# PV of both heads of a pair in one PSUM bank: 64 output rows each, three products side by side, and x split straight from PSUM

## The chip, the cores and the metric

The kernel runs on one core of a Trainium2 chip. The metric is device time in microseconds (us) of one execution. The core's engines work side by side, each on its own queue in order: TensorE (PE, with its weight loads PEld), VectorE (DVE), ScalarE (ACT), GpSimd (POOL) and the queue that issues the DMAs (SP). Results of PE land in PSUM, in banks of 512 fp32 columns on 128 partitions.

## The reference

Attention with a forget gate over 8 batches, 8 heads, 576 positions and head width 64, then a two-layer network with g = h cos(h) on the joined heads:

```python
scores = scale * np.matmul(q, k.transpose(0, 1, 3, 2))
cum = np.cumsum(np.log(np.clip(f, 0.0001, 1.0)), axis=-1)
scores = np.where(causal, -1000000000.0, scores + cum[:, :, :, None] - cum[:, :, None, :])
attn = np.exp(scores - np.max(scores, axis=-1, keepdims=True))
attn = attn / (np.sum(attn, axis=-1, keepdims=True) + 1e-09)
x = np.matmul(attn, v)            # (8, 8, 576, 64) -> x: (4608, 512)
h = x @ w_in                      # w_in (512, 2048)
out = (h * np.cos(h)) @ w_out     # w_out (2048, 512)
```

To keep fp32 accuracy the kernel splits an fp32 number into two fp16 numbers, hi and lo, and adds up products of the parts.

## The kernel before, in words

**Units.** Two heads make a pair; four pairs (n = 4b to 4b+3) make batch b, and there are 32 pairs. For each head `attention(n)` computes scores for five row blocks of 128 positions on PE (lines 621 and 622, fp32 operands), adds the mask and takes the row minimum of the negated scores on DVE (632), takes exp and its sum on ACT (637), forms the reciprocal of the sum on POOL and DVE (642, 645) and splits the normalized P into fp16 hi (654, ACT) and lo (658, DVE) in the SBUF tiles PS3 (row blocks 3 and 4) and PS2 (0, 1, 2). A transposing DMA (663) brings them into `pt3` and `pt2` with the key position on partitions.

**PV.** V of a pair is split into hi and lo in the tile `vv` (584, 586). The 576 positions are cut into two halves of 320 and 256 columns (`UW`). For each head and each half, lines 671 to 689 multiply: the stationary operand is `vv[:, jb, hd]` as 128 columns, 64 of V hi and 64 of V lo, and the moving operand is P hi and then P lo of that head. So a bank receives P times V hi in rows 0 to 63 and P times V lo in rows 64 to 127: all four products of the parts. For a half of 320 a head takes 8 matmuls of 64, 256, 256 and 128 columns, two of each; for a half of 256 it takes 10, eight of 256 and two of 128.

**Behind PV.** ACT copies rows 64 to 127 into the tile `low` (694). For the first six pairs (`n < NX`) ACT also copies rows 0 to 63 into `x32` (698) and POOL adds `low` (700); from the seventh pair on DVE does scale and addition in one instruction that reads the bank (703). When both heads of a half are there, ACT casts `x32` to fp16 (713: xh) and POOL subtracts (715: xl).

**The network.** For each of 16 units u (a half of a batch) `gemm1` multiplies xh and xl with the split w_in (735), ACT brings h out of PSUM (740), DVE and ACT compute h cos(h) (749, 751, 753, 755) and split it (757 gh, 758 gl), and `gemm2` multiplies with the split w_out (775), whose result leaves through ACT (780) and a DMA. The weights come as 64-bit numbers; DVE puts fp32 words together from them at the start (428, 432, 436), ACT takes their sums (447), and after a maximum over partitions (`allmax`, 380 to 385) each block of 512 columns is split: hi on ACT (456), lo on DVE (463) or on POOL (460 and 461).

**What sets the order.** All operations are recorded with an engine, a cost and a priority. `Plan.order()` then runs a list scheduler over them 20 times, forward and backward in turn, and keeps the shortest plan; the program's order on each engine is that plan's. An operation with `alt` is put on DVE or on POOL by which would finish it earlier in the plan: lines 574 and 575 (`sub`), 463 against 460 and 461, and 758. Rings of buffers (`BUFS`) limit how far work runs ahead: `pa1` has three PSUM banks that scores and PV share, `hp` three banks for the network (and, in the first three pairs, for the second head), `x32` and `low` one buffer each.

The loop at the end of the kernel advances a pair's generator by pieces:

```python
        adv(n)
        if p == 2 and b + 1 < B:
            prep_vscale(b + 1, float(n))
        adv(n)
        adv(n + 1)
        adv(n)
```

Of the kernel before, what the change touches and what calls it, by code (L numbers as in the profile page):

```python
# [13 lines left out]
F32 = mybir.dt.float32  # L14
F32R = mybir.dt.float32r
F16 = mybir.dt.float16
BF16 = mybir.dt.bfloat16
I32 = mybir.dt.int32
AF = mybir.ActivationFunctionType
ALU = mybir.AluOpType  # L20
# [4 lines left out]
P = 128  # L25
B, H, S, D = 8, 8, 576, 64
# [4 lines left out]
U0, UW = (0, 320), (320, 256)  # L31
NU = len(UW)
UM = max(UW)
QP = 640
NSET = 3
OFF = {0: 0, 1: 128, 2: 384, 3: 0, 4: 512}
# [1 line left out]
VS0 = -3.0  # L38
RAWS = {1: ("h",), 2: ("gh", "gl")}
SLQ, SLW, SLG = 2.0, 2.0, 0.0  # L40
NX = 6
LEAD = 2.0
NHP = 3
ROUNDS = 20
SWITCH = 4.0
TWO_PI = 2.0 * np.pi
NEG = -8.0e9
BUFS = dict(stage=2, x32=1, v2=2, vv=2, pt3=2, pt2=2, low=1, xh0=6, xl0=6, xh1=7, xl1=7, h=3, r=1, gh=5, gl=5, ot=1,
            pa2=1, pa1=3, hp=3, dg=1)


# [62 lines left out]
class Plan:  # L114
# [14 lines left out]
    def op(self, eng, cost, fn, reads=(), writes=(), prio=0.0, size=0, table=None, alt=None):  # L129
        o = Op()  # L130
        o.eng, o.cost, o.size, o.table, o.fn, o.prio, o.alt, o.id = eng, cost, size, table, fn, prio, alt, len(self.ops)
        deps = {}
        for b in reads:
            if b.last is not None:
                deps[b.last.id] = b.last
        for b in writes:
            if b.last is not None:
                deps[b.last.id] = b.last
            for r in b.readers:
                deps[r.id] = r  # L140
        for b in (*reads, *writes):
            r = b.root()
            assert not r.closed, r.name
            if r.wait:
                r.wait.closed = True
                for w in r.wait.ops:
                    deps[w.id] = w
            if r.prev is not None and r.prev.ops:
                deps[r.prev.ops[0].id] = r.prev.ops[0]
            r.ops.append(o)  # L150
        for b in reads:
            b.readers.append(o)
        for b in writes:
            b.last, b.readers = o, []
        deps.pop(o.id, None)
        o.deps, o.succ, o.n, o.ready = list(deps.values()), [], len(deps), 0.0
        for d in o.deps:
            d.succ.append(o)
        self.ops.append(o)
        return o  # L160
# [121 lines left out]
def c_dve(n, fast=False, k=1):  # L282
    return k * 0.064 + n * (0.53e-3 if fast else 1.06e-3)


def c_act(n, psum=False, aps=0):
    return (0.052 if psum else 0.093) + n / 1200.0 + 0.093 * aps


def c_pool(n):  # L290
    return 0.06 + n * 2.6e-3


def c_mm(n):
    return max(0.028, n / 2400.0 + 0.0025)
# [7 lines left out]
def fox_moe_kernel(ctx: ExitStack, tc: tile.TileContext, qkT, vp, fT, w1, w2, out):  # L303
# [51 lines left out]
    def ring(name, shape, dt, space=pool, tag=None):  # L355
        tag = tag or name
        return pl_.ring(tag, lambda: space.tile(shape, dt, name=tag, bufs=BUFS[tag]))

# [13 lines left out]

    def allmax(src, n, reads, dst, writes, pr):

        dg = ring("dg", [P, n, P], BF16, tag="dg" if n == 1 else "x32")
        pm = ring("hp", [P, 512], F32, psum)

        def spread():
            for j in range(n):
                V.tensor_scalar(dg.get()[:, j], eye, src()[:, j:j + 1], None, op0=ALU.mult)  # L380

        op("DVE", 0.2 * n, spread, reads=reads, writes=[dg], prio=pr)
        op("PE", c_mm(n * P) + 0.1, lambda: T.matmul(pm.get()[:, 0:n * P], ones, dg.get().rearrange("p n c -> p (n c)"), start=True, stop=True),
           reads=[dg], writes=[pm], prio=pr)
        op("DVE", c_dve(n * P), lambda: V.tensor_reduce(dst(), pm.get()[:, 0:n * P].rearrange("p (n c) -> p n c", n=n), axis=AX.X, op=ALU.max),
           reads=[pm], writes=writes, prio=pr)
# [166 lines left out]
    def attention(n):  # L553
# [37 lines left out]
        for hd in range(2):  # L591
# [11 lines left out]
            for tag, blocks in GROUPS:  # L603
# [10 lines left out]
                def mm(blocks=blocks, big=big, view=view, hi=hi, co=co):  # L614
                    for ib, o, w in blocks:
                        isl = slice(ib * P, ib * P + P)
                        hf = S // 2
                        d_ = view(ib, o, w)
                        for c, d in ((d_[:, 0], slice(0, hf)), (d_[:, 1], slice(hf, S))) if big else ((d_, slice(0, w)),):
                            d = slice(64 + d.start, 64 + d.stop)  # L620
                            T.matmul(c, hi[:, 0, isl], hi[:, 1, d], start=True, stop=False)  # L621
                            T.matmul(c, co[0:68, 0, isl], co[0:68, 1, d], start=False, stop=True)  # L622
# [42 lines left out]
                       reads=[PB[ib, hl] for ib in ibs for hl in range(2)], writes=[t], prio=pr + 0.2, size=int(nblk * 0.112 * DMA_BW))  # L665
            yield

        x32 = ring("x32", [P, S], F32)
        for hd in range(2):
            hs = slice(64 * hd, 64 * hd + 64)  # L670
            for half in range(NU):
                b0, w = U0[half], UW[half]
                pv = ring("hp" if n < NHP and hd == 1 else "pa1", [P, 512], F32, psum)
                t = (T2, T3)[half][hd]
                if half == 0:
                    jobs = [(0, 0, 0, 1, 64), (0, 64, 1, 3, 0), (1, 64, 1, 3, 0), (2, 192, 2, 3, 0)]
                else:
                    jobs = [(0, 0, 0, 2, 0), (1, 0, 0, 2, 0), (2, 0, 0, 2, 0), (3, 0, 0, 2, 0), (4, 128, 1, 2, 0)]

                def mm(pv=pv, t=t, jobs=jobs, hd=hd, half=half, w=w):  # L680
                    for k, (jb, o, i0, i1, c0) in enumerate(jobs):
                        first = k == 0 or (half == 0 and k == 1)
                        for hl in range(2):
                            bl = [OFF[3 * half + i] // P + jb for i in range(i0, i1)]
                            m = t.get()[:, hl, bl[0]:bl[-1] + 1:bl[-1] - bl[0] or 1, c0:]
                            o1 = o + (i1 - i0) * (P - c0)
                            d = pv.get()[:, o:o1].rearrange("p (a c) -> p a c", a=i1 - i0)
                            T.matmul(d, vv.get()[:, jb, hd].rearrange("p h d -> p (h d)"), m,  # L688
                                     start=(first and hl == 0), stop=(hl == 1 and (k == len(jobs) - 1 or (half == 0 and k == 0))))

                rd_ = [t, vv.part(0), vv.part(1)]
                op("PE", sum(2 * (c_mm((i1 - i0) * (P - c0))) for _, _, i0, i1, c0 in jobs) + 0.02, mm, reads=rd_, writes=[pv], prio=pr + 0.6)
                low, ls = ring("low", [P, UM], F32), hs if n < NX else slice(0, 64)
                op("ACT", c_act(w, True), lambda pv=pv, low=low, w=w, ls=ls: A.activation(
                    low.get()[ls, 0:w], pv.get()[64:128, 0:w], AF.Copy, scale=float(2.0 ** -14)), reads=[pv], writes=[low], prio=pr + 0.6)
                xp = x32.part((half, hd))
                if n < NX:
                    op("ACT", c_act(w, True), lambda pv=pv, hs=hs, b0=b0, w=w: A.activation(
                        x32.get()[hs, b0:b0 + w], pv.get()[0:64, 0:w], AF.Copy, scale=float(2.0 ** -14)), reads=[pv], writes=[xp], prio=pr + 0.6)
                    op("POOL", c_pool(w) + 0.06, lambda low=low, hs=hs, b0=b0, w=w: G.tensor_tensor(  # L700
                        x32.get()[hs, b0:b0 + w], x32.get()[hs, b0:b0 + w], low.get()[hs, 0:w], op=ALU.add), reads=[low], writes=[xp], prio=pr + 0.6)
                else:
                    op("DVE", c_dve(w), lambda pv=pv, low=low, hs=hs, b0=b0, w=w: V.scalar_tensor_tensor(
                        x32.get()[hs, b0:b0 + w], pv.get()[0:64, 0:w], float(2.0 ** -14), low.get()[0:64, 0:w], op0=ALU.mult, op1=ALU.add),
                       reads=[pv, low], writes=[xp], prio=pr + 0.6)
            if hd == 0:
                yield
        X.setdefault(n, [])
        for half in range(NU):
            b0, w = U0[half], UW[half]  # L710
            xh, xl = ring(f"xh{half}", [P, w], F16), ring(f"xl{half}", [P, w], F16)
            x3 = [x32.part((half, hd)) for hd in range(2)]
            op("ACT", c_act(w), lambda xh=xh, b0=b0, w=w: A.copy(xh.get(), x32.get()[:, b0:b0 + w]), reads=x3, writes=[xh],  # L713
               prio=pr + 0.6)
            op("POOL", c_pool(w), lambda xh=xh, xl=xl, b0=b0, w=w: G.tensor_tensor(xl.get(), x32.get()[:, b0:b0 + w], xh.get(), op=ALU.subtract),  # L715
               reads=[*x3, xh], writes=[xl], prio=pr + 0.6)
            X[n].append((xh, xl))

    GT = {}

# [142 lines left out]
```

## Time and profile before

| | |
|---|---|
| time, median of 3 runs | 1196.62 us (1196.18 to 1203.8) |
| profiled execution, its own time | 1195.68 us |
| its span, first to last instruction | 1194.0 us |
| PE busy | 1020.9 us, 86% |
| ACT busy | 936.1 us, 78% |
| DVE busy | 881.4 us, 74% |
| POOL busy | 400.5 us, 34% |
| mean granted TensorE clock | 0.947 |

The span and the profiled execution's own time differ by 1.7 us, so what is read from the span holds for the time. A matmul's duration in the profile is its latency; matmuls overlap, and their rate is read from a stretch of many of them. Rows of the groups give busy us and mean ns of one instruction, then the idle time just before it and what ended that. A row of the stretches gives the time from and to, its length, busy us with the number of instructions for PE, PEld, DVE, ACT and POOL, the granted clock, the DMA share and GB/s. A row of the waits gives who waited for whom, us in total, how often, and the longest.

### The profile page before, as it was taken

The numbers are of one execution on the slowest core, as the hardware profiler recorded it, in microseconds if no ns is written. First come the engines' busy times: TensorE is split into PE (matmuls) and PEld (weight loads), VectorE is DVE, ScalarE is ACT, GpSimd is POOL, SyncE is SP. The second block draws the span as 40 slices with busy tenths as digits, with TensorE's granted clock in tenths as the row PEclk, the third lists the DMA queues.
The fourth block names the chain that finished last, engine by engine and source line by source line (L and its number), as shares of the span: only waits on it lengthen the run. The fifth ranks groups of instructions, "written<-read, shape, count | busy, mean of one in ns | idle before, by whom it ended". The sixth has DMA issues, their size and how long they took to land. (4 is left out here: it accounts for less than half of the span.)

```text
span 1194.0 us, 22292 instructions
## 1 busy us (share of the span) xinstructions
PE 1020.9 (86%) x8077; PEld 826.3 (69%) x8077; DVE 881.4 (74%) x1879; ACT 936.1 (78%) x1922; POOL 400.5 (34%) x460
## 2 busy tenths in 40 slices
PE   1354348898999799989999899989989899999998
PEld 1243236677877687778877687777777777788777
DVE  4999997978578775878587866869497877863613
ACT  2688668999789887999699977989699888973523
POOL 3436667742422411253125221441135222200000
PEclk9975569999999999999999899999999999999999
DMA  9999834584637843696449544784459564440000
GB/s 256 276 281 274 219 89 82 134 200 99 152 77 192 191 85 70 156 197 141 104 97 232 122 100 81 169 209 102 88 134 205 111 152 103 84 78 15 6 23 19
DMA packets 291070, 161.25 MB, mean 135 GB/s; under 512 B 255056, under 2 KB 263248, under 8 KB 290960
## 3 DMA queue, kind: packets, MB, share of 16 engines
q1 hardware_dynamic: 290960, 159.83, 57.5%
q8 instruction: 63, 1.03, 0.4%
q14 instruction: 47, 0.39, 0.1%
HBM read 76.82 MB, written 10.62 MB: 73 GB/s over the span
## 5 line engine op out<-in xcount | busy, mean ns | idle before, releaser
L735 PE MATMUL hp<-xh,W1s 128*128 128x256 f16 (+1 forms) x2048 | 390.9, 290 | 16.6 <-ACT h L740 11.5
L775 PE MATMUL hp<-gh,W2s 128*128 128x256 f16 (+1 forms) x2048 | 381.9, 287 | 3.9 <-ACT h L740 3.3
L735 PEld LDWEIGHTS <-W1s 128*128 128x128 f16 x3072 | 298.3, 99 | 109.0 <-issue 30.5
L775 PEld LDWEIGHTS <-W2s 128*128 128x128 f16 x3072 | 296.4, 98 | 79.2 <-issue 5.3
L735 PE MATMUL hp<-xl,W1s 128*128 128x256 f16 (+1 forms) x1024 | 296.5, 290 | 2.2 <-POOL xl L715 2.2
L775 PE MATMUL hp<-gl,W2s 128*128 128x256 f16 (+1 forms) x1024 | 293.3, 286 | 0.3 <-DVE gl L758 0.2
L642 POOL TENSOR_SCALAR ri<-L 128x2 f32<-128x2 f32 (+1 forms) x192 | 67.7, 353 | 361.9 <-ACT pa L637 350.0
L658 DVE SCALAR_TENSOR_TENSOR PS<-pa,ri,PS 128x64 f16<-128x64 f32 (+4 forms) x308 | 154.6, 545 | 36.0 <-ACT PS L654 35.0
L637 ACT ACTIVATE pa<-pa,nb 128x64 f32<-128x64 f32 (+4 forms) x308 | 155.6, 505 | 26.9 <-DVE nb L632 24.9
L688 PEld LDWEIGHTS <-vv 128*128 128x128 f16 x1152 | 107.0, 103 | 85.7 <-issue 53.2
L632 DVE CUSTOM_DVE_ANT_0 pa<-pa,mask 128x64 f32<-128x64 f32 (+4 forms) x308 | 146.8, 507 | 24.9 <-PE pa L622 23.9
L621 PE MATMUL pa<-QK 128*128 128x448 f32 (+2 forms) x372 | 125.9, 350 | 45.3 <-DVE PS L658 32.1
L688 PE MATMUL pa<-pt,vv 128*128 128x64 f16 x1098 | 123.2, 262 | 46.5 <-DMA pt<-PS 19.5
L654 ACT ACTIVATE PS<-pa,ri 128x64 f16<-128x64 f32 (+4 forms) x308 | 150.3, 540 | 12.2 <-DMA pt<-PS 3.2
L740 ACT ACTIVATE h<-hp 128x320 f32<-128x320 f32 (+1 forms) x256 | 102.3, 414 | 55.7 <-PE hp L735 54.0
L575 POOL TENSOR_TENSOR QC<-stage,QK 64x576 fp32r<-64x576 f32 x61 | 93.3, 1529 | 121.3 <-ACT QK L569 120.3
L621 PEld LDWEIGHTS pa<-QK 128*128 128x128 f32 x372 | 77.4, 208 | 77.4 <-issue 56.5
L755 DVE TENSOR_TENSOR h<-h,r 128x1280 f32<-128x1280 f32 (+1 forms) x64 | 89.2, 1393 | 51.8 <-ACT r L753 51.3
L622 PE MATMUL pa<-QC 68*128 68x448 f32 (+2 forms) x372 | 107.1, 325 | 2.0 <-DMA QC<-cum_d 2.0
L758 DVE TENSOR_TENSOR gl<-h,gh 128x1280 f16<-128x1280 f32 (+1 forms) x64 | 94.9, 1482 | 14.8 <-ACT gh L757 14.8
L574 POOL TENSOR_TENSOR QK<-stage,QK 64x576 fp32r<-64x576 f32 x63 | 99.1, 1573 | 16.4 <-ACT QK L569 10.8
L715 POOL TENSOR_TENSOR xl<-x,xh 128x320 f16<-128x320 f32 x64 | 61.8, 968 | 124.3 <-ACT xh L713 122.2
(110 smaller groups left out, 1325.4 us busy)
## 6 DMA issues: line engine op xcount, KB each, us to landing
stage<-in_dram SPq DMA_DIRECT2D x64, 576.0 KB
v<-in_dram SPq DMA_DIRECT2D x32, 320.0 KB
QC<-QK SPq DMA_DIRECT2D x64, 144.0 KB
stage<-in_dram SPq DMA_DIRECT2D x28, 320.0 KB
h<-in_dram SPq DMA_DIRECT2D x16, 512.0 KB
out_dram<-ot SPq DMA_DIRECT2D x32, 160.0 KB
gh<-in_dram SPq DMA_DIRECT2D x16, 256.0 KB
gl<-in_dram SPq DMA_DIRECT2D x16, 256.0 KB
```

The costliest lines, as they stand in the source:

```text
L574: sub(lambda e: e.tensor_tensor(hi[up, 0, ks], qk.get()[up, 0], hi[up, 0, ks], op=ALU.subtract), [qk, x["hi"]], [x["ql"]])
L621: T.matmul(c, hi[:, 0, isl], hi[:, 1, d], start=True, stop=False)
L622: T.matmul(c, co[0:68, 0, isl], co[0:68, 1, d], start=False, stop=True)
L632: op("DVE", c_dve(w) + 0.008, lambda view=view, ib=ib, o=o, w=w, mk=mk, c=c: V.tensor_tensor_reduce(out=view(ib, o, w), in0=view(ib, o, w) ...
L637: op("ACT", c_act(w, True, 2), lambda view=view, ib=ib, o=o, w=w, c=c: A.activation(view(ib, o, w), view(ib, o, w), AF.Exp, bias=nb.get()[ ...
L654: op("ACT", c_act(w, True, 1), lambda view=view, ib=ib, o=o, w=w, c=c, out_=out_: A.activation(out_(0), view(ib, o, w), AF.Copy, scale=ri. ...
L658: op("DVE", c_dve(w) + 0.06, lambda view=view, ib=ib, o=o, w=w, c=c, out_=out_: V.scalar_tensor_tensor(out_(1), view(ib, o, w), ri.get()[: ...
L688: T.matmul(d, vv.get()[:, jb, hd].rearrange("p h d -> p (h d)"), m, start=(first and hl == 0), stop=(hl == 1 and (k == len(jobs) - 1 or (h ...
L735: T.matmul(hp.get()[:, 0:w_], WS_[1][:, 4 * c + cb, w, fs], x.get(), start=(n == 0), stop=(n == 11))
L740: op("ACT", c_act(w_, True), lambda hp=hp, k=k: A.activation(h.get()[:, k, 0:w_], hp.get()[:, 0:w_], AF.Copy, scale=float(2.0 ** -24)), re ...
L758: op("DVE", c_dve(N), lambda: V.tensor_tensor(fl(gl), fl(h), fl(gh), op=ALU.subtract), reads=[*hk, gh], writes=[gl], prio=pr, alt=("POOL", ...
L775: T.matmul(po.get()[:, 0:w_], WS_[2][:, 4 * c + k, w, msl], g.get()[:, k, 0:w_], start=(n == 0), stop=(n == 47))
```

## The change

PV of a half is now one operation for both heads. The stationary operand is 64 columns, V hi or V lo of one head, and the output of head 0 goes to rows 0 to 63 of a bank, that of head 1 to rows 64 to 127. Three products are added in the same rows: V hi with P hi, V hi with P lo, V lo with P hi; V lo with P lo is left out. The matmuls of the two heads alternate. A half of 320 has 24 matmuls, a half of 256 has 30: 54 for a pair where there were 36.

The bank then holds x of both heads. ACT casts it to xh straight from PSUM, and DVE computes xl as the scaled bank minus xh. The copies to `low` and `x32`, the additions on DVE or POOL and the subtraction on POOL are gone, and so are these two tiles. `pt3` has three buffers instead of two, `xh1` and `xl1` six instead of seven, and the four-column maximum uses a buffer of `gh`. PV waits for the transposed P of both heads and for both parts of `vv`. Line numbers of the changed kernel are lower by 1 up to about line 665 and by 19 from `gemm1` on; its PV is line 686, xh line 692, xl line 694.

```diff
-NX = 6
-BUFS = dict(stage=2, x32=1, v2=2, vv=2, pt3=2, pt2=2, low=1, xh0=6, xl0=6, xh1=7, xl1=7, h=3, r=1, gh=5, gl=5, ot=1,
+BUFS = dict(stage=2, v2=2, vv=2, pt3=3, pt2=2, xh0=6, xl0=6, xh1=6, xl1=6, h=3, r=1, gh=5, gl=5, ot=1,
             pa2=1, pa1=3, hp=3, dg=1)
...
-        dg = ring("dg", [P, n, P], BF16, tag="dg" if n == 1 else "x32")
+        dg = ring("dg", [P, n, P], BF16, tag="dg" if n == 1 else "gh")
...
-        x32 = ring("x32", [P, S], F32)
-        for hd in range(2):
-            hs = slice(64 * hd, 64 * hd + 64)
-            for half in range(NU):
-                b0, w = U0[half], UW[half]
-                pv = ring("hp" if n < NHP and hd == 1 else "pa1", [P, 512], F32, psum)
-                t = (T2, T3)[half][hd]
...
-                            T.matmul(d, vv.get()[:, jb, hd].rearrange("p h d -> p (h d)"), m,
-                                     start=(first and hl == 0), stop=(hl == 1 and (k == len(jobs) - 1 or (half == 0 and k == 0))))
...
-                if n < NX:
-                    op("ACT", c_act(w, True), lambda pv=pv, hs=hs, b0=b0, w=w: A.activation(
-                        x32.get()[hs, b0:b0 + w], pv.get()[0:64, 0:w], AF.Copy, scale=float(2.0 ** -14)), reads=[pv], writes=[xp], prio=pr + 0.6)
-                    op("POOL", c_pool(w) + 0.06, lambda low=low, hs=hs, b0=b0, w=w: G.tensor_tensor(
...
-                else:
-                    op("DVE", c_dve(w), lambda pv=pv, low=low, hs=hs, b0=b0, w=w: V.scalar_tensor_tensor(
...
         for half in range(NU):
             b0, w = U0[half], UW[half]
+            pv = ring("hp" if n < NHP else "pa1", [P, 512], F32, psum)
...
+            def mm(pv=pv, jobs=jobs, half=half):
+                for k, (jb, o, i0, i1, c0) in enumerate(jobs):
+                    first = k == 0 or (half == 0 and k == 1)
+                    last = k == len(jobs) - 1 or (half == 0 and k == 0)
+                    bl = [OFF[3 * half + i] // P + jb for i in range(i0, i1)]
+                    o1 = o + (i1 - i0) * (P - c0)
+                    for x, (kv, kp) in enumerate(((0, 0), (0, 1), (1, 0))):
+                        for hd in range(2):
+                            m = (T2, T3)[half][hd].get()[:, kp, bl[0]:bl[-1] + 1:bl[-1] - bl[0] or 1, c0:]
+                            d = pv.get()[64 * hd:64 * hd + 64, o:o1].rearrange("p (a c) -> p a c", a=i1 - i0)
+                            T.matmul(d, vv.get()[:, jb, hd, kv], m, start=first and x == 0, stop=last and x == 2)
+
+            vp_ = list(vv.parts.values())
+            op("PE", sum(3 * c_mm((i1 - i0) * (P - c0)) for _, _, i0, i1, c0 in jobs) + 0.3, mm, reads=[*(T2, T3)[half], *vp_], writes=[pv],
+               prio=pr + 0.6)
             xh, xl = ring(f"xh{half}", [P, w], F16), ring(f"xl{half}", [P, w], F16)
-            x3 = [x32.part((half, hd)) for hd in range(2)]
-            op("ACT", c_act(w), lambda xh=xh, b0=b0, w=w: A.copy(xh.get(), x32.get()[:, b0:b0 + w]), reads=x3, writes=[xh],
-               prio=pr + 0.6)
-            op("POOL", c_pool(w), lambda xh=xh, xl=xl, b0=b0, w=w: G.tensor_tensor(xl.get(), x32.get()[:, b0:b0 + w], xh.get(), op=ALU.subtract),
-               reads=[*x3, xh], writes=[xl], prio=pr + 0.6)
+            op("ACT", c_act(w, True), lambda pv=pv, xh=xh, w=w: A.activation(xh.get(), pv.get()[:, 0:w], AF.Copy, scale=float(2.0 ** -14)),
+               reads=[pv], writes=[xh], prio=pr + 0.6)
+            op("DVE", c_dve(w), lambda pv=pv, xh=xh, xl=xl, w=w: V.scalar_tensor_tensor(
+                xl.get(), pv.get()[:, 0:w], float(2.0 ** -14), xh.get(), op0=ALU.mult, op1=ALU.subtract), reads=[pv, xh], writes=[xl], prio=pr + 0.6)
             X[n].append((xh, xl))
+            if half == 0:
+                yield
```

The order of the program around the change follows from the plan. The matmuls of a pair's first half (320 columns), late in the program, on PE; `pa_...` is the bank, `pt_...` the transposed P, and the weight load ahead of each matmul is named by its tile. Before, one head:

```order
L775 MATMUL hp<-gl,W2s 128x320
L688 LDWEIGHTS vv
L688 MATMUL pa_8875<-pt_8749,vv 128x64
L688 LDWEIGHTS vv
L688 MATMUL pa_8875<-pt_8749,vv 128x64
L688 LDWEIGHTS vv
L688 MATMUL pa_8875<-pt_8749,vv 128x256
```

In the changed kernel the same place of a pair has two `pt` buffers in turn, one for each head:

```order
L756 MATMUL hp<-gl,W2s 128x320
L686 LDWEIGHTS vv
L686 MATMUL pa_8805<-pt_8561,vv 64x64
L686 LDWEIGHTS vv
L686 MATMUL pa_8805<-pt_8749,vv 64x64
L686 LDWEIGHTS vv
L686 MATMUL pa_8805<-pt_8561,vv 64x64
L686 LDWEIGHTS vv
L686 MATMUL pa_8805<-pt_8749,vv 64x64
```

What was two runs of 8 full-width matmuls per half is one run of 24 that write 64 rows each, between the same kinds of neighbours.

On DVE, just ahead of the first unit's polynomial (749 before, 730 now), in the stage in which weights are still split (463, now 462). Before:

```order
L632 ISA nb 128x1
L463 SCALAR_TENSOR_TENSOR W1s<-W1s,s_102 128x512
L544 TENSOR_SCALAR m_o_1402<-kw,vr 128x1
L536 TENSOR_SCALAR m_inv<-r_103,vr 128x4
L537 TENSOR_SCALAR m_a_1496<-m_inv 128x4
L538 TENSOR_SCALAR m_b_1497<-s_102,vs 128x4
L645 RECIPROCAL ri<-ri 128x2
L544 TENSOR_SCALAR m_o_1498<-kw,vr 128x1
L645 RECIPROCAL ri<-ri 128x2
L463 SCALAR_TENSOR_TENSOR W2s<-W2s,t_104 128x512
L749 TENSOR_SCALAR r<-h,m_a_1400 128x1280
```

In the changed kernel:

```order
L694 SCALAR_TENSOR_TENSOR xl_1466<-pa_1360,xh_1434 128x256
L631 ISA pa_1439,nb<-pa_1439,mask 128x192
L631 ISA nb 128x1
L585 SCALAR_TENSOR_TENSOR vv<-v_1170,vs,vv 128x10x64
L631 ISA pa_1471,nb<-pa_1471,mask 128x2x288
L631 ISA nb 128x1
L462 SCALAR_TENSOR_TENSOR W1s<-W1s,s_102 128x512
L644 RECIPROCAL ri<-ri 128x2
L462 SCALAR_TENSOR_TENSOR W2s<-W2s,t_104 128x512
L644 RECIPROCAL ri<-ri 128x1
L462 SCALAR_TENSOR_TENSOR W2s<-W2s,t_104 128x512
```

Ahead of that first polynomial DVE now has 8 subtractions for xl and 14 weight splits where it had none and 10; in the whole program it has 18 splits instead of 14, POOL 14 instead of 18. On POOL, late in the program, the xl between the subtractions for Q and K (574, 575) has gone. Before:

```order
L575 TENSOR_TENSOR QC_82<-stage,QK_79 64x576
L574 TENSOR_TENSOR QK_79<-stage,QK_79 64x576
L715 TENSOR_TENSOR xl_8985<-x_8788,xh_8967 128x320
L575 TENSOR_TENSOR QC_83<-stage,QK_80 64x576
L574 TENSOR_TENSOR QK_80<-stage,QK_80 64x576
```

In the changed kernel:

```order
L574 TENSOR_TENSOR QC_82<-stage,QK_79 64x576
L573 TENSOR_TENSOR QK_79<-stage,QK_79 64x576
L641 TENSOR_SCALAR ri<-L 128x2 x2
L641 TENSOR_SCALAR ri<-L 128x1
L573 TENSOR_TENSOR QK_80<-stage,QK_80 64x576
```

What stands behind POOL's xl before stands one place earlier now, and DVE has the xl in its own order.

More of the change, by code (lines that the diff above doesn't have):

```diff
@@ L666, in attention @@
             yield
-        x32 = ring("x32", [P, S], F32)
-        for hd in range(2):
-            hs = slice(64 * hd, 64 * hd + 64)
-            for half in range(NU):
-                b0, w = U0[half], UW[half]
-                pv = ring("hp" if n < NHP and hd == 1 else "pa1", [P, 512], F32, psum)
-                t = (T2, T3)[half][hd]
-                if half == 0:
-                    jobs = [(0, 0, 0, 1, 64), (0, 64, 1, 3, 0), (1, 64, 1, 3, 0), (2, 192, 2, 3, 0)]
-                else:
[L678 to L688, printed above, removed]
-                                     start=(first and hl == 0), stop=(hl == 1 and (k == len(jobs) - 1 or (half == 0 and k == 0))))
[L691 to L696, printed above, removed]
-                if n < NX:
-                    op("ACT", c_act(w, True), lambda pv=pv, hs=hs, b0=b0, w=w: A.activation(
-                        x32.get()[hs, b0:b0 + w], pv.get()[0:64, 0:w], AF.Copy, scale=float(2.0 ** -14)), reads=[pv], writes=[xp], prio=pr + 0.6)
[L700 to L707, printed above, removed]
@@ new lines, in attention @@
+            if half == 0:
+                jobs = [(0, 0, 0, 1, 64), (0, 64, 1, 3, 0), (1, 64, 1, 3, 0), (2, 192, 2, 3, 0)]
+            else:
+                jobs = [(jb, 128 if jb == 4 else 0, jb // 4, 2, 0) for jb in range(5)]
+            def mm(pv=pv, jobs=jobs, half=half):
[9 more added lines that the diff above has]
+                            T.matmul(d, vv.get()[:, jb, hd, kv], m, start=first and x == 0, stop=last and x == 2)
@@ L717, in attention @@
             X[n].append((xh, xl))
+            if half == 0:
+                yield
     GT = {}
```

## The prediction

> **What bounds the kernel now.** I read the page first, then the busy time in six stretches, then PE's waits, then the chain of waits that ended last. The page's engine rows and the granted clock in 40 slices (rows of the page):
>
> ```profile
> PE 1020.9 (86%) x8077; PEld 826.3 (69%) x8077; DVE 881.4 (74%) x1879; ACT 936.1 (78%) x1922; POOL 400.5 (34%) x460
> PEclk9975569999999999999999899999999999999999
> ```
>
> The shares are means over two very different stages, as the stretches show:
>
> ```profile
> 0.00:40.00 40.00, 7.25 (x25) 6.31 (x26) 24.29 (x59) 15.84 (x34) 12.60 (x31) 1.00 0.93 281
> 40.00:170.00 130.00, 53.82 (x247) 41.42 (x247) 128.50 (x329) 93.91 (x239) 75.54 (x79) 0.63 0.86 224
> 170.00:210.00 40.00, 33.29 (x230) 24.21 (x230) 32.32 (x64) 34.23 (x70) 27.48 (x24) 0.93 0.44 94
> 210.00:600.00 390.00, 364.83 (x2986) 297.33 (x2986) 295.24 (x625) 340.97 (x682) 141.01 (x154) 0.99 0.61 138
> 600.00:1060.00 460.00, 431.90 (x3495) 350.40 (x3494) 344.38 (x753) 397.95 (x813) 140.97 (x172) 0.98 0.60 132
> 1060.00:1194.00 134.00, 129.80 (x1100) 106.61 (x1097) 56.69 (x54) 53.19 (x88) 2.95 (x3) 1.00 0.08 21
> ```
>
> From 40 to 170 us DVE is busy for 128.50 of 130 us: it sets the start, and PE, at a clock of 0.63, waits. From 210 to 1060 us PE is busy for 796.7 of 850 us (364.83 + 431.90) and sets the time. From 1060 on there is almost only the network on PE. So an us less of PE work after 210 is worth about an us; ACT and DVE work there is worth only what PE waits for them; and DVE work before 170 is worth about its own time, since all PE work behind it moves with it.
>
> The 53.3 us in which PE is idle between 210 and 1060 are nearly all in these rows of the waits of that stretch (columns: us in total, times, longest):
>
> ```profile
> PE pa L688 <- DVE PS L658: 11.8, 13, 2.8
> PE hp L735 <- ACT h L740: 10.6, 9, 3.0
> PE pa L621 <- DVE PS L658: 9.8, 7, 4.7
> PE pa L621 <- DVE x L703: 4.8, 4, 1.4
> PE pa L688 <- DMA pt<-PS: 4.1, 5, 1.8
> PE hp L735 <- ACT ot L780: 3.3, 2, 1.8
> PE hp L775 <- ACT h L740: 3.3, 2, 3.0
> PE hp L735 <- ACT xh L713: 1.7, 2, 1.1
> PE hp L735 <- POOL xl L715: 1.6, 2, 1.1
> ```
>
> The last three pieces needed are the rate of PE at full clock, from the chain of waits (start, us, what):
>
> ```profile
> 1038.09 0.98 PE pa L688 x10
> 1043.53 0.61 PE pa L688 x8
> 1169.68 20.97 PE hp L775 x192
> ```
>
> 192 matmuls of 256 columns in 20.97 us are 109 ns each, loads hidden. 8 x 109 ns + 2 x 54 ns = 0.98: a product of 128 columns takes about 55 ns in a run. And 0.61 - 4 x 0.109 - 2 x 0.055 = 0.064 for the two products of 64 columns, about 30 ns each: even there a full-width fp16 load is hidden.
>
> **PE, the product itself.** A pair costs 2 x (0.61 + 0.98) = 3.18 us now. How many pairs lie where PE sets the time:
>
> ```profile
> 170.00:210.00 40.00, 2.69 (x26) 2.27 (x26) 0.93 0.44 94
> 210.00:1060.00 850.00, 100.40 (x946) 83.31 (x946) 0.99 0.60 135
> 1060.00:1194.00 134.00, 3.52 (x36) 3.00 (x36) 1.00 0.08 21
> ```
>
> These are the PV matmuls alone, 36 to a pair: 1008 / 36 = 28 pairs.
>
> No row shows two matmuls side by side, so the price needs bounds. If the two heads overlap wholly and loads stay hidden, a half of 320 takes three times 0.030 + 0.109 + 0.109 + 0.055 = 0.91, a half of 256 three times 4 x 0.109 + 0.055 = 1.47: 2.38 a pair, 0.80 less, -22 us over 28 pairs. If they don't overlap it is twice that, 4.76, +1.58 a pair, +44 us. Between them stand the loads: there are now two for each step. The nearest rows are two matmuls on fp32 operands in one run, the first of 64 columns (start, duration):
>
> ```profile
> 243.43 0.28 PE L622 MATMUL pa<-QC 68*128 68x64 f32 x1
> 243.54 0.39 PE L621 MATMUL pa<-QK 128*128 128x320 f32 x1
> ```
>
> The next starts 0.11 us later, not 0.03: there the load of 128 columns sets the pace, at 0.11. Two loads of 64 columns are as many columns, so if the load of a half-width operand goes at that pace, each step has a floor of 0.11: steps of 64 and 128 columns rise to it, those of 256 already have it. A half of 320 takes 3 x (0.11 + 0.109 + 0.109 + 0.11) = 1.31, a half of 256 3 x (0.436 + 0.11) = 1.64: 2.95 a pair, 0.23 less, **-6.4 us** over 28 pairs. If the fp16 pace (30 ns a load, 60 for two) holds, the steps are nearly the streams' and the sum is nearer -22. I take -6.4, since splitting a load is more likely to lose pace than to keep it. The Trainium skill, "TensorEngine Tiling (Array Packing)", section on tile-to-partition mapping, restrictions, says that column tiling turns fast weight load off; by that rule the floor, and not the fp16 pace, is the price; no run here shows it yet.
>
> Both columns of heads need their 64-row outputs in one bank, so PV of a pair can only begin when the second head's transposed P is there. Queued behind it on PE are whole runs of the network (12 matmuls of 109 ns or more for each operation), and the order puts PV late enough for that; a third `pt3` buffer gives it room. I cost this at 0 to +4 us, the size of the row for PV's wait on the transposing DMA, and take 0 within the next term.
>
> **ACT, DVE and POOL after 210.** Rows by shape (us in total, mean ns of one, idle before):
>
> ```profile
> L694 ACT ACTIVATE low<-pa 64x320 f32<-64x320 f32 x61 | 26.5, 434 | 3.6 <-PE pa L688 2.3
> L694 ACT ACTIVATE low<-pa 64x256 f32<-64x256 f32 x61 | 23.2, 381 | 9.5 <-PE pa L688 8.4
> L713 ACT CAST xh<-x 128x320 f16<-128x320 f32 x32 | 14.6, 457 | 4.6 <-POOL x L700 2.5 <-DVE x L703 1.9
> L713 ACT CAST xh<-x 128x256 f16<-128x256 f32 x32 | 13.1, 410 | 3.3 <-DVE x L703 3.3
> L703 DVE SCALAR_TENSOR_TENSOR x<-pa,low 64x320 f32<-64x320 f32 x52 | 24.9, 480 | 18.9 <-ACT low L694 18.2
> L703 DVE SCALAR_TENSOR_TENSOR x<-pa,low 64x256 f32<-64x256 f32 x52 | 21.6, 416 | 9.7 <-ACT low L694 8.9
> ```
>
> From the seventh pair on, ACT drops 2 x (0.434 + 0.381) + 0.457 + 0.410 = 2.50 us a pair and gets two reads of a bank, which `low` prices at 0.434 + 0.381 = 0.82: 1.68 less. DVE drops 2 x (0.480 + 0.416) = 1.79 and gets xl, one read of a bank and one of SBUF as line 703 has, 0.90: 0.90 less. Over some 26 pairs that is 44 us of ACT's 739 and 23 us of DVE's 640 in this stretch. None of it is on the path by itself. It shortens PE's waits: the rows for L703, xh and xl (8.1 us in all) are for steps that go or change; one read less in the chain should halve them, -4. The rows behind ACT's h and ot and DVE's PS (11.8 + 10.6 + 9.8 + 3.3 + 3.3 = 38.8) are queueing; ACT's idle share rises from 111 of 850 us to 155 and DVE's from 210 to 233, and I take a sixth of them, -6. Together **-10 us**. The ends: -20, if queueing falls as ACT's idle time rises (by two fifths), and +5, if banks come free later, since a bank is now held through a cast on ACT and then a pass on DVE, as it was through `low` and line 703 before.
>
> **The start.** Here nothing goes from DVE, since the first six pairs used ACT and POOL. DVE gets 8 xl ahead of the first unit's polynomial, 8 x (0.480 + 0.416) / 2 = +3.6, and four splits more (the order shows 14 for 10):
>
> ```profile
> L463 DVE SCALAR_TENSOR_TENSOR W1s<-W1s,s 128x512 f16<-128x512 f32 x7 | 8.7, 1242 | 0.0
> L463 DVE SCALAR_TENSOR_TENSOR W2s<-W2s,t 128x512 f16<-128x512 f32 x7 | 6.1, 868 | 0.1
> L461 POOL TENSOR_TENSOR W1s<-W1s 128x512 f16<-128x512 f32 x9 | 12.7, 1412 | 0.7
> L460 POOL TENSOR_TENSOR W1s<-W1s,s 128x512 f32<-128x512 f32 x9 | 10.8, 1195 | 9.4 <-ACT W1s L456 9.0 <-DVE W2s L432 0.3
> ```
>
> 4 x (1.242 + 0.868) / 2 = +4.2: +7.8 us on the engine that sets this stage. Against it, POOL loses work up to 170 us: its additions (700), its subtractions (715), and four pairs of 460 and 461 at 2.61 us, 10.4. In rows of their own, POOL's lines 700 and then 715:
>
> ```profile
> 0.00:170.00 170.00, 16.70 (x16) 0.71 0.88 237
> 0.00:170.00 170.00, 8.37 (x8) 0.71 0.88 237
> ```
>
> That is 35.5 us of POOL, and POOL's work slows DVE's. The same subtraction gl over the whole span, where POOL is busy 34%, and after 1080 us, where it does nothing:
>
> ```profile
> L758 DVE TENSOR_TENSOR gl<-h,gh 128x1280 f16<-128x1280 f32 x32 | 53.0, 1657 | 6.9 <-ACT gh L757 6.9
> L758 DVE TENSOR_TENSOR gl<-h,gh 128x1280 f16<-128x1280 f32 x4 | 6.0, 1489 | 2.6 <-ACT gh L757 2.6
> ```
>
> 11% for 34% of POOL: about 0.33 us of DVE for one us of POOL, -11.7 for 35.5, or about -8 as a third of DVE's work there reads banks. Sum of the start: **0 us**, between -8 and +8.
>
> **Sum.** 1195.68 - 6.4 - 10 + 0 = 1179.3 by the profiled execution, which lies 0.9 below the median of the runs: 1180 us.
>
> **Rivals.**
> *The heads don't overlap.* PE runs 54 half-width matmuls one behind the other: +44 on PE, -6 or less from lighter ACT and DVE: about 1232. For it: no row shows an overlap. Against it: the operands and the rows written are disjoint. By the Trainium skill, "TensorE: Matmul & The Clock Gate", part 3, column-packed matmuls do run concurrently (three 32-row ones gave 2.38 times); no run here shows it.
>
> *PE drains at each change of width.* Each PV operation stands between full-width runs, so PE would have to empty before and after it. The shortest PV matmul, which is about its latency, is in the row of line 688 (min/median/max):
>
> ```profile
> L688 PE MATMUL pa<-pt,vv x1098: 189/272/421, 46.5 to 1072.0; 128*128 128x64 f16 x61, 128*128 128x128 f16 x61, 128*128 128x256 f16 x61
> ```
>
> Four halts of 0.19 a pair are 0.76 x 28 = +21, so PE is 15 dearer, not 6 cheaper; with -5 on the waits, about 1206: slower. It decides from 0.06 us a halt on, where the 0.23 are gone. For it: all PV runs have such neighbours in the order; against it: the fp32 products on 68 rows, between others on 128, start 0.11 apart without a gap. "TensorEngine Tiling (Array Packing)", key properties, in the Trainium skill says that a change of tiling mode drains TensorE; if so, this rival's time is the one.
>
> *The start is late and the waits stay.* POOL's relief doesn't reach DVE, +8 at the start, waits unchanged, PE -6: about 1198, no change.
>
> *Streams set all the steps.* -22 on PE, -10: about 1164.
>
> **Chances.** Forecast (1170 to 1190) 0.42; streams 0.13; drain 0.20; late start 0.12; no overlap 0.13. A measurement tells about 1% from no change, 12 us. Faster by over 1% (under 1184.7) is the streams and nearly nine tenths of the forecast's share: 0.50. Slower by over 1% (over 1208.6) is no overlap and half of drain: 0.23. Between: 0.27. The range leaves out the far end of no overlap (0.12) and a little below: 1162 to 1222.
>
> **What would show it.** In the profile after: the chain or the stretches with a PV run of 30 matmuls in 1.64 us (1.5 if streams set it, 3 if nothing overlaps) and of 24 in 1.31; starts of the two heads a few ns apart; a gap of 0.2 us ahead of and behind PV if PE drains. ACT 1.7 and DVE 0.9 us a pair less; PE's idle time between 210 and 1060 about 43 us, with line 703's rows gone. The first unit's matmuls no later than before; the splits on DVE nearer to 0.87 than 1.24 us. Wrong it would be if PE waits for both heads' P, or if the start is late by more than 8 us.

## The result, and the profile after

The changed kernel takes 1213.72 us (median of four runs, 1210.62 to 1217.27) against 1198.3 us for the kernel before beside it: a ratio of 1.0125, 95% interval 1.0098 to 1.0152. It is slower by 15 us where 16 us less was forecast. The profiled execution took 1217.27 us with a span of 1215.5 us, 21.5 us more than the span shown before, so the rows below overstate the loss a little.

The engine rows and the granted clock of the page after:

```profile
PE 1019.7 (84%) x8653; PEld 823.1 (68%) x8653; DVE 851.4 (70%) x1841; ACT 867.7 (71%) x1766; POOL 307.6 (25%) x366
PEclk9976569998999899999999899988999789999999
```

ACT lost 68 us of work, DVE 30, POOL 93, and PE is busy for as long as before; still the kernel became slower. The stretches, as before:

```profile
40.00:170.00 130.00, 43.99 (x313) 34.02 (x311) 124.51 (x336) 78.27 (x203) 47.17 (x48) 0.68 0.88 225
170.00:210.00 40.00, 35.74 (x278) 26.67 (x278) 35.46 (x65) 37.16 (x75) 24.47 (x22) 0.93 0.43 80
210.00:600.00 390.00, 359.85 (x3134) 291.75 (x3133) 277.67 (x597) 311.92 (x617) 108.82 (x123) 0.97 0.62 137
600.00:1060.00 460.00, 424.11 (x3644) 341.67 (x3643) 323.50 (x692) 358.42 (x724) 113.63 (x137) 0.94 0.57 128
1060.00:1215.50 155.50, 146.93 (x1260) 120.84 (x1259) 64.41 (x84) 64.03 (x117) 1.16 (x6) 0.99 0.12 29
```

Between 210 and 1060 us PE is busy for 784.0 us where it was busy for 796.7, so it idles 13 us more; and the granted clock over these 850 us falls from 0.985 to 0.954 (weighted by the two rows), worth about 26 us of PE at full clock (an estimate: 850 x 0.031). So 155 us of the span lie after 1060 where 134 did before. Who PE waited for between 210 and 1060:

```profile
PE pa L686 <- DMA pt<-PS: 45.3, 16, 10.6
PE pa L620 <- DVE ri L644: 5.3, 3, 2.1
PE pa L620 <- DVE PS L657: 4.3, 7, 1.2
PE hp L716 <- ACT h L721: 2.6, 4, 1.1
```

One row leads now: PV waits 45.3 us for transposed P, 4.1 before. The rows behind ACT's h and ot and DVE's PS, on which the forecast wanted to save 6 us, did fall, from 38.8 to 10.0 us (with the small ones that aren't listed here).

**What PV costs now.** A stretch of PE's timeline at full clock (start, duration, then what; the number behind x is how many matmuls the row merges):

```profile
328.86 0.30 PE L716 MATMUL hp<-xl,W1s 128*128 128x320 f16 x1
329.09 1.11 PE L686 MATMUL pa<-pt,vv 128*64 128x64 f16 x24
330.13 0.47 PE L620 MATMUL pa<-QK 128*128 128x448 f32 x1
...
334.51 0.30 PE L716 MATMUL hp<-xl,W1s 128*128 128x320 f16 x1
334.74 1.67 PE L686 MATMUL pa<-pt,vv 128*64 128x256 f16 x30
336.34 0.45 PE L716 MATMUL hp<-xh,W1s 128*128 128x320 f16 x2
```

A matmul of 320 columns takes 0.136 us in a run (24.45 us for 180 at the end of the chain), so PV starts 0.09 to 0.10 us late: 329.09 instead of 329.00, 334.74 instead of 334.65. (In the kernel before, PV's first matmul starts 0.136 us after a matmul of 320 columns, without such a delay.) From its start to the next instruction the run of 24 takes 1.04 us and the run of 30 takes 1.60: the streams of one head alone (0.91 and 1.47) and about 0.1 us more. So the two heads do run side by side, at the pace of the streams, and each run has a halt of about 0.1 us ahead of it and one behind it. A pair costs 1.14 + 1.70 = 2.84 us instead of 3.18: 0.34 less, 9.5 us over 28 pairs. The PE term was won.

**Where P is late.** The third pair of a batch, its second half (256 columns), and the fourth pair behind it, in the changed kernel's timeline:

```profile
391.69 1.64 PE L686 MATMUL pa<-pt,vv 128*64 128x256 f16 x29 [0.64 <-DMA pt<-PS]
409.02 0.27 PE L716 MATMUL hp<-xl,W1s 128*128 128x256 f16 x1
409.36 0.19 PE L686 MATMUL pa<-pt,vv 128*64 128x64 f16 x1
411.82 0.36 ACT L692 ACTIVATE xh<-pa 128x256 f16<-128x256 f32 x1
415.10 1.93 PE L686 MATMUL pa<-pt,vv 128*64 128x64 f16 x23 [5.55 <-DMA pt<-PS]
420.35 3.09 PE L686 MATMUL pa<-pt,vv 128*64 128x256 f16 x30
```

PV of that half is over at 393.3 us, but ACT casts it out of its bank only at 411.82, 18.5 us later, 2.5 us behind the end of the last network matmul on the 256 columns of the batch before (409.02). The ring `xh1` has six buffers now: the third pair of a batch needs the one of the first pair of the batch before, and that is read until then. Until then one of the three `pa1` banks is shut and the fourth pair's scores have two; its P is late, and PE stands for 5.55 us at 409 to 415. That the shut bank is what makes this P late is an argument; no row shows it by itself. Both PV runs behind it go at half speed (1.93 instead of 1.08 us for 23 matmuls, 3.09 instead of 1.67). The bank is shut in the same way from 529.5 to 548.5 us and from 660.2 to 676.9 us, and in the third pair of every batch but the first, for 11 to 24 us. Before, the ring had seven buffers, and PV left its bank for `x32` anyway.

Every one of the 16 waits behind the 45.3 us looks like the one at 409.36: one matmul, of the first head, has run, and the second one, of the other head, waits. So what PE waits for is always the second head's P.

### The profile page after: what moved, and what is told of

It reads as the page before. It is cut to its first block, busy times and chain, and to the rows that moved or that the text cites. A ratio compares the mean times of both kernels' runs of the same rounds, so it can differ in the third digit from the quotient of the medians.

```text
span 1215.5 us, 23085 instructions
## 1 busy us (share of the span) xinstructions
PE 1019.7 (84%) x8653; PEld 823.1 (68%) x8653; DVE 851.4 (70%) x1841; ACT 867.7 (71%) x1766; POOL 307.6 (25%) x366
## 3 DMA queue, kind: packets, MB, share of 16 engines
q8 instruction: 68, 1.11, 0.4%
## 5 line engine op out<-in xcount | busy, mean ns | idle before, releaser
L641 POOL TENSOR_SCALAR ri<-L 128x2 f32<-128x2 f32 (+1 forms) x192 | 63.5, 331 | 510.3 <-ACT pa L636 431.0
L636 ACT ACTIVATE pa<-pa,nb 128x320 f32<-128x320 f32 (+4 forms) x308 | 156.0, 508 | 42.6 <-DVE nb L631 38.7
L686 PEld LDWEIGHTS <-vv 128*64 128x64 f16 x1728 | 94.8, 126 | 122.6 <-issue 104.6
L620 PE MATMUL pa<-QK 128*128 128x448 f32 (+2 forms) x372 | 132.1, 365 | 44.4 <-DVE PS L657 37.6
L686 PE MATMUL pa<-pt,vv 128*64 128x256 f16 (+2 forms) x1566 | 98.9, 280 | 80.2 <-DMA pt<-PS 73.2
L574 POOL TENSOR_TENSOR QC<-stage,QK 64x576 fp32r<-64x576 f32 x61 | 98.8, 1619 | 167.6 <-ACT QK L568 166.6
L620 PEld LDWEIGHTS pa<-QK 128*128 128x128 f32 x372 | 81.2, 218 | 78.4 <-issue 34.8
L621 PE MATMUL pa<-QC 68*128 68x448 f32 (+2 forms) x372 | 112.5, 338 | 3.5 <-DMA QC<-cum_d 2.5
L730 DVE TENSOR_SCALAR r<-h,m_a 128x1280 int32<-128x1280 f32 (+1 forms) x64 | 57.8, 903 | 71.0 <-ACT h L721 70.2
```

The costliest lines, as they stand in the source:

```text
L574: sub(lambda e: e.tensor_tensor(co[lo_, 1, ks], qk.get()[lo_, 1], hi[lo_, 1, ks], op=ALU.subtract), [qk, x["hi"]], [x["kl"]])
L636: op("ACT", c_act(w, True, 2), lambda view=view, ib=ib, o=o, w=w, c=c: A.activation(view(ib, o, w), view(ib, o, w), AF.Exp, bias=nb.get()[ ...
L686: T.matmul(d, vv.get()[:, jb, hd, kv], m, start=first and x == 0, stop=last and x == 2)
```

## The experiments

Theory **ring**: the change paid for the third `pt3` buffer with the seventh `xh1` and `xl1` buffer, and that is what costs, by way of the bank that stays shut. Rivals: **both heads** (PV of a pair must wait for the second head's P, whatever the buffers), **plan** (the planner takes P to land too early and puts PV too early), and that the matmuls don't overlap.

### One buffer more, and its control

The room for the seventh buffer comes from the second `v2` buffer.

```diff
-BUFS = dict(stage=2, v2=2, vv=2, pt3=3, pt2=2, xh0=6, xl0=6, xh1=6, xl1=6, ...
+BUFS = dict(stage=2, v2=1, vv=2, pt3=3, pt2=2, xh0=6, xl0=6, xh1=7, xl1=7, ...
```

> The changed kernel with xh1 and xl1 at seven buffers again, paid for by one v2 buffer instead of two. Theory ring: with six buffers the third pair's second half can't leave its PSUM bank until the network has done with the batch before (in the changed kernel's trace the bank was held from 391.7 to 411.8 us, from 528 to 548.5 and from 658.5 to 676.9), scores are left with two banks, P of the fourth pair comes late, and PE waits at PV. With seven it is gone: PE's waits on the transposed P after 210 us fall from 45 us to under 20, time about 1178 us, 1.5% under the kernel before. Theory both heads: PV of a pair has to wait for the second head's P whatever the ring, waits stay at 35 to 45 us and the time between 1203 and 1214 us.

Measured: 1189.97 us, ratio to the kernel before 0.9941 (0.9921 to 0.9960). The control changes `v2` alone:

> The control: the changed kernel with one v2 buffer instead of two and nothing else, xh1 and xl1 still at six. Theory ring: the third pair's second half still sits in its bank for about 18 us in each batch, waits on the transposed P 35 us or more, time about 1210 us, within 0.7% of the changed kernel. If the one v2 buffer were what helps, it would be as fast as the run with seven buffers.

Measured: 1215.17 us, 1.0140 (1.0104 to 1.0176), the same as the changed kernel. So the one buffer, with the order that the planner makes of it, is worth 25 us, 2%, and `v2` nothing. PE's timeline and ACT's cast at the same place of a batch; the control first, then seven buffers:

```profile
527.70 1.64 PE L686 MATMUL pa<-pt,vv 128*64 128x256 f16 x29 [3.39 <-DMA pt<-PS]
545.45 0.37 ACT L692 ACTIVATE xh<-pa 128x256 f16<-128x256 f32 x1
549.20 1.43 PE L686 MATMUL pa<-pt,vv 128*64 128x64 f16 x23 [4.66 <-DMA pt<-PS]
```

```profile
522.23 1.67 PE L686 MATMUL pa<-pt,vv 128*64 128x256 f16 x30
525.47 0.38 ACT L692 ACTIVATE xh<-pa 128x256 f16<-128x256 f32 x1
541.77 1.08 PE L686 MATMUL pa<-pt,vv 128*64 128x64 f16 x23 [0.66 <-DMA pt<-PS]
```

At this place the bank is held for 16 us with six buffers and for under 2 us with seven, and the fourth pair's PV waits 0.66 us instead of 4.66. The waits on P in all, between 210 and 1060, control and then seven:

```profile
PE pa L686 <- DMA pt<-PS: 35.0, 18, 10.8
```

```profile
PE pa L686 <- DMA pt<-PS: 26.6, 13, 9.5
```

The expectation of under 20 us and of 1178 us was missed. And the place shown is a favourable one. With seven buffers the third pair's bank is read out 1 to 6 us after its PV in every batch after the first, with six in the control after 12 to 24 us. But between 210 and 1060 the first halves of the fourth pairs wait for P no less with seven, 22 us in all, than with six, 20 us; one wait with seven is

```profile
679.58 1.93 PE L686 MATMUL pa<-pt,vv 128*64 128x64 f16 x23 [9.54 <-DMA pt<-PS]
```

and the difference in time arises late. Two stretches of the control, then of seven buffers:

```profile
210.00:900.00 690.00, 643.65 (x5594) 517.56 (x5593) 500.98 (x1056) 545.13 (x1089) 186.50 (x211) 0.98 0.61 136
900.00:1000.00 100.00, 82.22 (x720) 68.44 (x718) 61.79 (x158) 72.29 (x157) 25.04 (x33) 0.88 0.60 139
```

```profile
210.00:900.00 690.00, 643.88 (x5599) 518.91 (x5600) 495.41 (x1064) 556.22 (x1101) 176.21 (x209) 0.97 0.61 137
900.00:1000.00 100.00, 92.97 (x833) 76.15 (x828) 69.66 (x170) 83.18 (x177) 31.97 (x36) 0.98 0.68 155
```

At 900 us the two are level (4205 and 4188 network matmuls done); in the next 100 us, with one wait of 10.76 us at a fourth pair, the control falls 113 matmuls behind, and between 1060 and 1100 us another 52, where the third pair's bank of the last batch is shut for 24 us (1 us with seven). So that the shorter ring costs 25 us is shown; that it costs them through the fourth pair's P once in each batch is not, and the way from the shut bank to the time stays in part open.

### The kernel before with six buffers

```diff
-... xh1=7, xl1=7, h=3, ...
+... xh1=6, xl1=6, h=3, ...
```

> The kernel before with xh1 and xl1 at six buffers instead of seven and nothing else changed. Theory ring: it is slower too, by 10 to 40 us (the copy in x32 frees the bank, but x32 itself is one buffer, so the next pair's PV stops), about 1220 us. Theory both heads: no change within 0.5%, since each head's PV still goes by itself.

Measured: 1250.02 us, 1.0424 (1.0392 to 1.0456): 52 us slower, more than expected; so a short ring costs in both kernels. The rest of the change therefore wins 36 us where both have six buffers (1250 to 1214), and 8 us where both have seven (1198 to 1190): without `x32` the kernel is less hurt by a short ring, but a short ring hurts it still. PE's longest waits in that run are scores behind line 645 on DVE, PV behind the lo part of P, and scores behind line 703, which empties a bank:

```profile
PE pa L621 <- DVE ri L645: 20.2, 4, 5.2
PE pa L688 <- DVE PS L658: 17.3, 15, 3.4
PE pa L621 <- DVE x L703: 10.7, 5, 2.9
```

### The same products, not side by side

```diff
-                    for x, (kv, kp) in enumerate(((0, 0), (0, 1), (1, 0))):
-                        for hd in range(2):
+                for hd in range(2):     # around the loop over the jobs
+                        for x, (kv, kp) in enumerate(((0, 0), (0, 1), (1, 0))):
```

> The run with seven buffers, in the same planned order, but within a PV operation all products of head 0 come first and then all of head 1, so that two matmuls in a row write the same rows. If it is the alternation of the heads that lets two matmuls run side by side, a run of 30 takes about 3.0 us instead of 1.6 and one of 24 about 1.9 instead of 1.0: 2.2 us a pair, 60 us over 28 pairs, less what covers waits: 1225 to 1240 us. If PE pairs matmuls in any order, the time is that of the run with seven buffers.

Measured: 1215.53 us, 1.0139 (1.0114 to 1.0163), less than the 1225 to 1240 us expected. The two runs of a pair, from its timeline:

```profile
328.00 1.78 PE L686 MATMUL pa<-pt,vv 128*64 128x64 f16 x24
334.85 2.90 PE L686 MATMUL pa<-pt,vv 128*64 128x256 f16 x30
```

They take 1.78 and 2.90 us where 1.11 and 1.67 were taken side by side: the alternation of heads is what overlaps them, and 1.9 us a pair, 53 us over 28 pairs, is its worth on PE. The kernel lost 25.6 us. The other half was taken up by what PE had idled: between 210 and 1060 its idle time fell from 54 to 37 us (waits on P from 26.6 to 19.2), and the clock rose from 0.97 to 0.98. This is the clearest sign here that PE's own work is only part of the bound.

### The wait for both heads

In the kernel before, PV of the first head also reads the second head's P:

```diff
-                rd_ = [t, vv.part(0), vv.part(1)]
+                rd_ = [t, (T2, T3)[half][1], vv.part(0), vv.part(1)]
```

> The kernel before, where PV of the first head also waits for the second head's transposed P; matmuls, copies and buffers as before. It puts a price on the both-heads wait alone. Theory both heads: the waits on the transposed P after 210 us rise from 4 us (before) to 25 us or more, as in the run of the change with seven buffers (26.6 us), and the time rises by 12 to 30 us with the clock that is lost, to 1210 to 1228 us. If the wait is free because the network's matmuls fill it: 1196 to 1202 us.

Measured: 1254.93 us, 1.0490 (1.0459 to 1.0520). It is far slower, but not in the way that was expected: waits on P don't lead, waits for banks and x do, and the first network matmul comes at 189.0 us instead of 166.5:

```profile
PE pa L621 <- DVE x L703: 21.5, 10, 4.1
PE hp L735 <- ACT h L740: 15.4, 15, 2.9
PE hp L735 <- ACT xh L713: 9.6, 4, 2.7
```

With two `pt2` and two `pt3` buffers a wait for both heads keeps all of them shut; that is read from the code, not from a row. If so, this run doesn't price the wait, it prices the wait with too few buffers.

The next run has seven `xh1` buffers and all of `v2`, but two `pt3` buffers; both halves of a pair are recorded together for that (the `yield` between them goes).

> The change with xh1 and xl1 at seven, paid for in another way: both halves of a pair's PV are recorded together (no yield between them), so that pt3 needs two buffers, and v2 keeps its two. Theory ring: what matters is the seventh buffer and not v2 or pt3, so the time is near the other run with seven, 1185 to 1200 us, and clearly under the changed kernel's 1214. If the third pt3 buffer was needed for the joint wait, it is slower than 1205 us.

Measured: 1212.57 us, 1.0136 (1.0119 to 1.0152). The time near 1190 us was missed, and it came out as the expectation's other branch says, slower than 1205: seven buffers alone don't do it. Either the third `pt3` buffer or the order that the `yield` gives is worth about as much as the seventh x buffer; the run can't tell these two apart.

Last, in the change with seven buffers, PV of a half as two operations, one for each head, into the same bank:

```diff
-                op("PE", ..., mm, reads=[*(T2, T3)[half], *vp_], writes=[pv], ...)
+            for hd in range(2):
+                op("PE", ..., mm, reads=[(T2, T3)[half][hd], *vp_], writes=[pv.part(hd)], ...)
```

> The change with seven buffers, where PV of a half is two operations, one for each head, with 64 output rows into the same bank; so nothing runs side by side, as in the serial run (1215.5 us), but each head waits for its own P only. The difference to the serial run is the price of the both-heads wait within the change. Theory both heads: 12 us or more faster than the serial run, under 1204 us. If the wait costs nothing here: 1210 to 1222 us. If a half-filled bank that waits for its second head takes a bank from the scores, it is slower than 1222 us.

Measured: 1223.1 us, 1.0214 (1.0173 to 1.0255), to be held against the serial run's 1.0139. Letting each head go by itself gains nothing: it is about 0.7% slower. It lies just over the 1222 us that the expectation gave to a half-filled bank, too near to tell the two readings apart. Its waits on P are the lower ones:

```profile
PE pa L687 <- DMA pt<-PS: 16.2, 9, 2.6
```

So the expected gain from separate waits, 12 us or more, isn't there. That speaks against the both-heads theory as an account of the loss; it doesn't rule it out, since both runs compared have their products one after another, which covers waits, and each has an order of its own.

### A later landing in the plan

```diff
-                        s.ready = max(s.ready, end + (T_DMA1 if e == "SP" else LAT[e, s.eng]))
+                        s.ready = max(s.ready, end + (T_DMA1 + o.lag if e == "SP" else LAT[e, s.eng]))
```

with `o.lag` 2 us for transposing DMAs, and the same in the two places that go backward.

> The change with seven buffers, where the plan is told that a transposed P lands 2 us later than it assumed; nothing but the order changes. Theory plan: the waits that are left (26.6 us on the transposed P) come from a plan that puts PV too early, so PE gets network matmuls ahead of PV instead: waits under 12 us, clock 0.98 or more, time 1170 to 1182 us. If the waits come from too little work or too few buffers at the batch boundary, they stay and the time is 1188 us or more.

Measured: 1195.91 us, 0.9998 (0.9983 to 1.0014), against 0.9941 without. Waits on P fell from 26.6 to 13.9 us, as the plan theory said, but others came (line numbers in this run are higher by 1):

```profile
PE pa L621 <- DVE PS L658: 17.6, 14, 3.3
PE pa L687 <- DMA pt<-PS: 13.9, 5, 4.6
PE hp L717 <- ACT h L722: 8.4, 7, 2.9
PE pa L687 <- DVE xl L695: 6.0, 5, 2.5
```

> The control: the kernel before with the same later landing in its plan. Its PE hardly waits for the transposed P (4.1 us), so by either theory it gains nothing: 1194 to 1206 us.

Measured: 1215.73 us, 1.0164 (1.0148 to 1.0181); no change was expected. A later landing costs both kernels. The plan theory isn't borne out: fewer waits on P bought nothing. These two runs also show what an order alone can do: with no buffer and no instruction changed it moved the time by 0.6% and 1.6%.

### Two more on the version that is faster

> The change with seven buffers and a second buffer for the results that leave (ot), for which the room of the second v2 buffer still suffices. ACT waited 14 us for the DMA that empties the one ot buffer in the changed kernel. If ACT's queue is what the waits of PE hang on, it gains 3 us or more on the run with seven buffers (1190); if PE's clock and the waits on P are the rest, no change within 0.4%.

Measured, with `ot=2` on top of seven buffers: 1187.9 us, 0.9916 (0.9888 to 0.9944).

> The change with seven buffers, 60 rounds of the planner instead of 20; only the order can change. It shows how much of a difference of this size is the luck of a plan: 1180 to 1195 us expected; outside of that, differences under 1% between variants here can't be put down to their edits.

Measured: 1188.64 us, 0.9921 (0.9896 to 0.9947). Both beat the kernel before and the changed one; neither can be told from the run with seven buffers. So the kernels with seven x buffers, three `pt3` buffers and the heads side by side took 1188 to 1196 us in four different plans, and those with six 1214 and 1215 us in two: the 25 us are not the luck of one plan.

## Why the prediction was wrong

**PE, the product: right in sum, wrong in make-up.** -6.4 us was taken, and 0.34 us a pair, 9.5 us, is measured. The floor of 0.11 us for two loads isn't there: the runs go at the pace of the streams. "Streams set all the steps" would have been 0.80 a pair. Against it stands a halt as the drain rival has it, at half of its price: about 0.1 us instead of 0.19, four times a pair. The rule of the Trainium skill, "TensorEngine Tiling (Array Packing)", key properties, that a change of tiling mode drains TensorE, agrees with that 0.1 us; that the halt is a drain and nothing else isn't shown. The restriction in the same page's section on tile-to-partition mapping, that column tiling has no fast weight load, cost nothing that can be seen here. "TensorE: Matmul & The Clock Gate", part 3, on column-packed matmuls running concurrently, agrees: 1.67 us against 2.90 for the serial order of the same 30.

**The start: right within its bounds.** 0, between -8 and +8, was forecast. The first network matmul came at 160.4 us instead of 166.5. The make-up isn't shown: the splits on DVE took 1.05 us each in the mean, as before (1.06), and not the hoped-for 0.87, so the relief from less POOL work can't be seen there; that the sum held may be luck.

**The waits: the step that failed.** The term "together -10 us", with ends of -20 and +5, became 13 us more of idle PE and a clock worth some 26 us. That "the order puts PV late enough" didn't hold: PE waited 45.3 us for P. In two more places the working went past it. "A third `pt3` buffer gives it room" was read from the diff, but not what it was paid with: the same line takes `xh1` and `xl1` from seven to six, and no term was made for it. And "banks come free later ... held through a cast on ACT and then a pass on DVE, as it was through `low` and line 703 before" priced the copies and not the buffers that they need: in the kernel before, after 210 us, every bank was being read out by the last of its readers within 12 us of its PV, while now one in each batch waits for its xh1 buffer for 11 to 24 us. The runs with six and seven buffers put 25 us on the shorter ring, which is more than the whole loss.

**PV waits for both heads' P, 0 to +4:** 45.3 us were measured at that row, all of it for the second head's P, which the prediction had named as a sign of being wrong. With seven buffers 26.6 us are left. The runs don't part what the joint product adds from a P that is late anyway; the bound of 4 us was far too tight.

**ACT, DVE and POOL:** their work fell, by more than forecast: between 210 and 1060 ACT by 69 us, to 670 (44 forecast; part of it is that less of the work was done by 1060), DVE by 38, to 601 (23 forecast). The waits behind them fell too. PE's idle time rose all the same, at the one row of P.

**The rivals.** No overlap fell, and the start wasn't late. A halt as in the drain rival was seen, but it took less than the streams gave. None of the rivals was a ring of buffers that got shorter.

**What stays open.** With seven buffers PE still idles for 54 us between 210 and 1060, as much as the kernel before (53), and has a clock of 0.97 there against 0.985; of PE's 9.5 us, and of a start 1.6 us earlier (164.9), 8 us arrive, against 16 forecast. Which buffer or which order would bring the rest wasn't found: neither a later landing nor `ot` nor more rounds of planning did. Whether three `pt3` buffers or the order of recording is needed isn't settled either, nor how the shorter ring turns into 25 us when the two kernels are level up to 900 us.

## What to carry to other kernels

A line of buffer counts in a diff is an edit like any other: for each ring that gets shorter, look for the reader that ends last, and ask what the writer holds while it waits. Taking out an intermediate copy saves engine time, but it ties the resource ahead of the copy (here a PSUM bank) to the buffers behind it. A copy in between is no cure for a short ring, though: with six buffers the kernel that has it lost 52 us, the one without it 25. And where PE is busy nearly all the time, less work on the other engines is worth only what PE waits for them, while an operand that is late by some us also costs the clock behind it.

## What the runs showed of the hardware

Two matmuls with 64 output rows each, on different rows of one bank, ran wholly side by side: 30 of them, 24 of 256 columns and 6 of 128, in 1.60 us to the next instruction (334.74 to 336.34), as long as the two heads alternate; with one head after the other the same products took 2.90. In the run with one operation for each head, 15 of these matmuls, of one head alone, take the same 1.60 us:

```profile
333.19 1.67 PE L687 MATMUL pa<-pt,vv 128*64 128x256 f16 x15
334.79 0.45 PE L716 MATMUL hp<-xh,W1s 128*128 128x320 f16 x2
```

Going into such a run and out of it cost about 0.1 us each here.

A wait can cost more than itself. In the changed kernel, runs of 23 matmuls after waits of different lengths:

```profile
463.99 1.08 PE L686 MATMUL pa<-pt,vv 128*64 128x64 f16 x23 [1.43 <-DMA pt<-PS]
993.05 1.08 PE L686 MATMUL pa<-pt,vv 128*64 128x64 f16 x23 [1.88 <-DMA pt<-PS]
550.68 1.90 PE L686 MATMUL pa<-pt,vv 128*64 128x64 f16 x23 [4.46 <-DMA pt<-PS]
815.09 1.92 PE L686 MATMUL pa<-pt,vv 128*64 128x64 f16 x23 [5.87 <-DMA pt<-PS]
```

After up to 1.9 us of waiting the run is at full speed, after 4.5 us and more at little over half. In between it goes both ways: in the changed kernel the same run took 1.92 us after a wait of 2.78 us; in the control, 1.80 us after 2.07 us, but 1.08 us after 2.26 us. From 412 to 425 us, behind the wait of 5.55 us, the granted clock is 0.61:

```profile
412.00:425.00 13.00, 9.90 (x74) 7.98 (x74) 11.82 (x13) 8.05 (x12) 7.85 (x4) 0.61 0.59 105
```

"TensorE: Matmul & The Clock Gate" of the Trainium skill, part 1, has an idle window of about 3.4 us take TensorE to half clock. That agrees with the waits of 4.5 us and more; the waits of 2.07 and 2.78 us, with half speed behind them, are shorter than the page's figure.
